# Windowed attention and a gelu MLP on one core: the order of work from the first down product on as one list of single-engine steps, with named PSUM banks

## The chip, the core and the metric

One core of a Trainium2 chip. The metric is device time in microseconds (us) of one launch, as the median of the runs. The engines are TensorE (PE, matmuls), VectorE (DVE), ScalarE (ACT), GpSimd (POOL) and SyncE (SP, which here only issues transfers). Each engine runs its own instructions in the order in which the kernel emits them and waits where it needs another engine's result.

## The reference

```
# q, k, v: 8 batches x 8 heads x 576 positions x 64
scores = q @ k^T / 8, kept where 0 <= i - j < 64, else -1e9
a      = softmax(scores) @ v
x      = a, as 4608 tokens x 512        # heads side by side
h      = x @ w_in                       # 512 -> 2048
g      = h * sigmoid(1.702 h)
out    = g @ w_out                      # 2048 -> 512, float32
```

## The kernel before

Matmuls are in bf16 with float32 sums in PSUM. The 4608 tokens are 36 tiles m of 128 and nine chunks of 512. A tile is two blocks of 64 queries, and each block sees 128 keys.

**Attention of a tile.** `scores` (L302, tag c in the list) takes 16 small matmuls with 64 rows of contraction into the two banks of pool psS, or "apart" into two single banks. `exp` (L327, x) makes the exponentials on ACT, `mask` (L337, m) multiplies by the band on DVE, `pv` or `pv_two` (L355 and L373, v) multiplies by values for one or two tiles into psT, and `norm` or `norm_two` (L360 and L384, n) divides on DVE. The rows are then turned to columns: for tiles below 16 by PE and copies (`x_mm` L411, `x_out` L434), above it by a transposing DMA on SP's queue (`x_dma` L436, xd).

**Loads for attention.** Batches 0 to 2 are loaded as float32 and cast. From tile (2, 3) on `load_bf16` (L226, l) loads q, k and v with casting DMAs on POOL's queue. `turn_dma` (L237, y) turns q and k by DMA on SP's queue, and `shift_v` (L231, h) makes the copy of v that is offset by half a block, on POOL. `v_nat` and `v_off` have two buffers each, by the parity of the batch, so a load of v for batch b writes over that of b - 2.

**MLP.** `up_mm` (L444, u) multiplies x by a part of w_in into one bank. g comes out of it in one of two ways: `up_gelu` (L483) on ACT alone, or `up_th` (L462) on ACT and then `up_g` (L478) on DVE. An exp after a gelu needs another table on ACT (`soften`, L1086). Chunk 0 goes down by plain products (`down` L486). The later half-chunks q (2 to 17) go down by a scheme of seven block products in place of eight: `add_g` (L534, a) and `add_w` form sums, `product` (L552, p) does n = 1, 6, 7, 4 into one bank (the chain) and 2, 5, 3 into another (the part), `keep_chain` (L588, k) copies a state of the chain away, `add_out` (L591, o) and `last_of_chain` (L597, z) put together the output, and `store` (L581, s) sends it. The last chunk's up products use the same scheme: `up_product` (L655, F), `up_keep` (K), `up_add` (O), `up_last` (G).

**Order.** The scheduler is off: each engine's order is the order of the calls. Up to a point in chunk 1 and 2 it is a list of calls written by hand; after it comes a text, `plan` (L1024), with 727 tokens such as `p2.1` or `u34.t`, which a loop (`steps`, L1121) turns into calls. Most tokens stand for steps on several engines: `l` for three loads, `y` for two turns, `t` for turns on PE and their copies on ACT, `u…g` for an up product and its gelu.

**Banks.** PSUM has eight banks: psS and psT have two each as one buffer, psH and psO two buffers of one bank each. A new tile takes the next buffer of its pool in turn and waits until that buffer's last readers are done. Outputs take one of five buffers of `ob_pool` in the same way.

Of the kernel before, what the change touches and what calls it, by code (L numbers as in the profile page):

```python
# [29 lines left out]
def kernel(  # L30
# [20 lines left out]
    ob_pool = ctx.enter_context(tc.tile_pool(name="ob", bufs=5))  # L51
    psS = ctx.enter_context(tc.tile_pool(name="psS", bufs=1, space=bass.MemoryType.PSUM))
    psT = ctx.enter_context(tc.tile_pool(name="psT", bufs=1, space=bass.MemoryType.PSUM))
    psH = ctx.enter_context(tc.tile_pool(name="psH", bufs=2, space=bass.MemoryType.PSUM))
    psO = ctx.enter_context(tc.tile_pool(name="psO", bufs=2, space=bass.MemoryType.PSUM))
# [30 lines left out]
    def load_v(b, i, queue=None):  # L86
        (queue or nc.sync).dma_start(
            out=heads(stage_of_v(b, i)[0 : size(i), :]), in_=rows_of(v, b, i)
        )

    def cast_v(b, i, engine=None, parts=(0, 1, 2)):
        n, vn, vo = size(i), v_nat[b % 2], v_off[b % 2]
        src = heads(stage_of_v(b, i)[:])
        pieces = [
            (vo[64:128, i, :, 0:D], src[0:64]),
            (vn[0:n, i, :, 0:D], src[0:n]),
            (vo[0:64, i + 1, :, 0:D], src[64:128]) if i < 4 else None,
        ]
        for p in parts:
            if pieces[p]:  # L100
                (engine or nc.gpsimd).tensor_copy(out=pieces[p][0], in_=pieces[p][1])
# [4 lines left out]
    def load_qk(b, i):  # L106
        for w, src in enumerate((q, k)):
            nc.sync.dma_start(
                out=heads(stage_of_qk(b, i)[0 : size(i), w, 0:DM]), in_=rows_of(src, b, i)
            )  # L110
# [4 lines left out]
    def cast_qk(b, i):  # L115
        n = size(i)
        for w in range(2):
            nc.gpsimd.tensor_copy(
                out=rows[b % 2][w][0:n, i, :], in_=stage_of_qk(b, i)[0:n, w, 0:DM]
            )  # L120

    def load_quads(half):
        hs = slice(4 * half, 4 * half + 4)
        for w, src in enumerate((q, k)):
            nc.sync.dma_start(
                out=stage_qk[half][:, w, :].rearrange("p (h e) -> p h e", h=4),
                in_=src[0, hs, 0:512, :].rearrange("h (p r) d -> p h (r d)", r=4),
            )
# [37 lines left out]
    def load_pairs(b, i):  # L166
        n = pairs(i)
        for w, src in enumerate((q, k)):
            nc.sync.dma_start(
                out=stage_qk[(3 * b + i) % 2][0:n, w, :].rearrange("p (h e) -> p h e", h=H),  # L170
                in_=src[b, :, 256 * i : 256 * i + 2 * n, :].rearrange(
                    "h (p r) d -> p h (r d)", r=2
                ),
            )
# [17 lines left out]
    def turn_mm(b, i, w, tiles):  # L192
        n = pairs(i)
        for hp in range(4):
            for r in range(2):
                nc.tensor.transpose(  # L196
                    out=tiles[hp // 2][:, w, hp % 2, r, 0:n],
                    in_=pair_rows(b, i, w)[0:n, hp // 2, r, P * (hp % 2) : P * (hp % 2) + P],
                    identity=ident[0:n, 0:n],
                )  # L200

    def turn_out(b, i, w, tiles, half, engine):
# [6 lines left out]
            in_=tiles[half][:, w, :, :, 0:n].rearrange("p g r n -> p g n r"),  # L209
        )  # L210

    def turn_tiles():

        return [
            pool.tile([P, 2, 2, 2, P], bf16, name="turn", tag=tag)
            for pool, tag in ((psS, "S"), (psT, "T"))
        ]

# [7 lines left out]
    def load_bf16(b, i):  # L226
        for w, src in enumerate((q, k)):
            nc.gpsimd.dma_start(out=heads(row_block(b, i, w)), in_=rows_of(src, b, i))  # L228
        nc.gpsimd.dma_start(out=v_nat[b % 2][0 : size(i), i, :, 0:D], in_=rows_of(v, b, i))  # L229

    def shift_v(b, i):  # L231
        vn, vo = v_nat[b % 2], v_off[b % 2]
        nc.gpsimd.tensor_copy(out=vo[64:128, i, :, :], in_=vn[0:64, i, :, :])  # L233
        if i < 4:
            nc.gpsimd.tensor_copy(out=vo[0:64, i + 1, :, :], in_=vn[64:128, i, :, :])  # L235

    def turn_dma(b, i):  # L237
        n = size(i)
        for w in range(2):
            nc.sync.dma_start_transpose(  # L240
                out=qkt[b % 2][w][:, :, PAD + P * i : PAD + P * i + n],
                in_=row_block(b, i, w),
            )
# [15 lines left out]
    for half in range(2):  # L259
        load_quads(half)  # L260
    for i in (0, 2):
        load_v(0, i)
    ident = keep.tile([P, P], bf16, name="ident")
    nc.gpsimd.memset(ident[:], 0.0)
    nc.gpsimd.affine_select(
        out=ident[:], in_=ident[:], compare_op=ALU.not_equal, fill=1.0,
        base=0, pattern=[[-1, P]], channel_multiplier=1,
    )
    band = keep.tile([P, 64], bf16, name="band")
    nc.gpsimd.memset(band[:], 1.0)  # L270
    nc.gpsimd.affine_select(
        out=band[:], in_=band[:], compare_op=ALU.is_ge, fill=0.0,
        base=64, pattern=[[1, 64]], channel_multiplier=-1,
    )
    nc.gpsimd.affine_select(
        out=band[:], in_=band[:], compare_op=ALU.is_ge, fill=0.0,
        base=-1, pattern=[[-1, 64]], channel_multiplier=1,
    )
    for i in range(2):
        nc.vector.memset(qkt[i][1][:, :, 0:PAD], 0.0)  # L280
        nc.vector.memset(v_off[i][0:64, 0, :, :], 0.0)
        nc.vector.memset(v_nat[i][:, :, :, D : D + 2], 2.0)
        nc.vector.memset(v_off[i][:, 1:5, :, D : D + 2], 2.0)
        nc.vector.memset(v_off[i][64:128, 0, :, D : D + 2], 2.0)

    band_all = keep.tile([P, 1024], bf16, name="band_all")
    nc.vector.tensor_copy(
        out=band_all[:].rearrange("p (n c) -> p n c", c=64),
        in_=band[:].unsqueeze(1).to_broadcast([P, 16, 64]),
    )  # L290
    far = keep.tile([P, 512], bf16, name="far")
    nc.vector.tensor_scalar(
        out=far[:], in0=band_all[:, 0:512],
        scalar1=-1.0, scalar2=30000.0, op0=ALU.add, op1=ALU.mult,
    )
# [6 lines left out]
    def scores(m, masked=False, apart=False):  # L302

        if apart:
            st = [psH.tile([P, 512], fp32, name="S", tag="H")[:] for _ in range(2)]
# [67 lines left out]
    def pv_two(m):  # L373

        acc = psT.tile([P, 2, 512], fp32, name="Tacc", tag="T")
        rest = psH.tile([P, 2, 66], fp32, name="Tacc", tag="H")
# [27 lines left out]
    def x_dst(m):  # L404
        ch = m // 4
        if m % 4 == 0:
# [21 lines left out]
    def x_out_two(m):  # L428
        ps = X_of.pop(m)
        for i in range(2):  # L430
            nc.scalar.copy(out=x_dst(m + i), in_=ps[:, i])

    def x_out(m):
        nc.scalar.copy(out=x_dst(m), in_=X_of.pop(m)[:])  # L434
# [7 lines left out]
    turns = itertools.count()  # L442

    def up_mm(ch, f, nf, t0, nt, wide=False):  # L444

        pool, tag = (psO, "O") if wide and next(turns) % 2 else (psH, "H")
        ps = pool.tile([P, nf, nt], fp32, name="hps", tag=tag)

# [37 lines left out]
    def down(ch, tsub, j, pool=None, tag="O"):  # L486

        if j == 0:
            O_of[ch, tsub] = (pool or psO).tile([P, DM], fp32, name="ops", tag=tag)
# [9 lines left out]
    def down_out(ch, tsub, on_dve=False):  # L499
        o_sb = ob_pool.tile([P, DM], fp32, name="o_sb", tag="o_sb")  # L500
        ps = O_of.pop((ch, tsub))
        if on_dve:
            nc.vector.tensor_copy(out=o_sb[:], in_=ps[:])
        else:
            nc.scalar.copy(out=o_sb[:], in_=ps[:])
        eng = nc.sync if ch < 6 else nc.scalar
        eng.dma_start(out=out_tiled[:, ch * 4 + tsub, :], in_=o_sb[:])
# [40 lines left out]
    def bank(c, pr, at, name):  # L548
        pool, tag = (psO, "O") if (c, pr) != (NCH - 1, 1) else ((psS, "S"), (psT, "T"))[at]
        return pool.tile([P, 256], fp32, name=name, tag=tag)  # L550

    def product(c, pr, n):  # L552
# [8 lines left out]
        if n == 1:  # L561
            A_of[c, pr] = bank(c, pr, 0, "chain")
        if n == 2:
            C_of[c, pr] = bank(c, pr, 1, "part")
# [11 lines left out]
    def out_half(c, pr, t, n):  # L576
        if (c, pr, t) not in o_of:
            o_of[c, pr, t] = ob_pool.tile([P, DM], fp32, name="o_sb", tag="o_sb")
        return o_of[c, pr, t][:, 256 * n : 256 * n + 256]

    def store(c, pr, t, half=None):  # L581
        eng = nc.sync if c < 6 or half == 1 else nc.scalar
        cols = slice(0, DM) if half is None else slice(256 * half, 256 * half + 256)
        eng.dma_start(
# [6 lines left out]
    def add_out(c, pr, n):  # L591
        at, t, half = {2: (0, 0, 0), 5: (2, 1, 1), 3: (1, 0, 1)}[n]
        nc.vector.tensor_tensor(  # L593
            out=out_half(c, pr, t, half), in0=C_of[c, pr][:], in1=kept(c, pr, at), op=ALU.add
        )

    def last_of_chain(c, pr, engine):  # L597
        copy_on(engine, out=out_half(c, pr, 1, 0), in_=A_of.pop((c, pr))[:])
# [49 lines left out]
    rings = itertools.count()  # L648
    homes = {32: "ST", 33: "H", 34: "ST", 35: "H"}

    def up_bank(g, at):
        pool, tag = (psH, "H") if homes[g] == "H" else ((psS, "S"), (psT, "T"))[at]
        return pool.tile([P, 2, 256], fp32, name="up", tag=tag)[:]

    def up_product(g, n):  # L655
# [523 lines left out]
```

The softmax here doesn't subtract the row's maximum and nothing guards it: scores larger than these inputs give would overflow.

## Time and profile before

| | |
|---|---|
| median of 3 runs | 295.6 us (294.55 to 295.86) |
| span of the profiled execution | 293.0 us |
| around the span (295.6 less 293.0) | 2.6 us |
| PE / DVE / ACT / POOL busy | 283.5 / 195.5 / 181.1 / 141.3 us |
| granted PE clock | 0.998 |
| last matmul ends | 289.7 us |

The span is from the first to the last instruction of one execution; the median is of executions without the profiler. Busy time of PE includes matmuls whose ends are modelled, so the starts are read where tenths of a microsecond matter. The mean DMA busy share is 90% or more in nearly every fortieth of the span until about 220 us; after that it falls.

### The profile page before, as it was taken

The page shows a single profiled execution, that of the slowest core. Times are in us where ns is not written, and L with a number is a line of the kernel's source. Part 1 is how long each engine was busy: PE and PEld are TensorE (multiplying, and loading weights), DVE is VectorE, ACT ScalarE, POOL GpSimd, SP SyncE. Part 2 cuts the span into 40 slices and gives each one's busy share as a digit, 9 for nine tenths or more (in the row PEclk, how much of TensorE's full clock was granted, in tenths as well). Part 3 has the DMA queues.
Part 4 walks back from the last instruction along what each step waited for, and adds up shares of the span by engine and source line. Part 5 has one row for each costly group of instructions (what it writes and reads, how often), then busy time and mean ns, then how long its engine had stood idle before and what let it go on. Part 6 is the DMA issues. An engine that isn't in the chain of part 4 may idle for free.

```text
span 293.0 us, 8976 instructions
## 1 busy us (share of the span) xinstructions
PE 283.5 (97%) x3783; PEld 249.6 (85%) x3783; DVE 195.5 (67%) x377; ACT 181.1 (62%) x289; POOL 141.3 (48%) x191
## 2 busy tenths in 40 slices
PE   7899999999999999999999999999999999999995
PEld 6578555999898898889898999998899899989984
DVE  5667715898898685375636573756787864768771
ACT  3676534877775389776758746776657653556411
POOL 1570446744999999709569985078510000000000
PEclk9999999999999999999999999999999999999999
DMA  7999999996999999999999999999955171001233
GB/s 237 236 206 219 240 243 225 239 159 128 84 142 119 166 130 134 185 164 146 140 186 154 139 151 198 183 160 143 142 70 117 36 182 39 0 2 72 74 125 126
DMA packets 149768, 42.79 MB, mean 146 GB/s; under 512 B 135136, under 2 KB 144864, under 8 KB 149728
## 3 DMA queue, kind: packets, MB, share of 16 engines
q0 software_dynamic: 77712, 13.64, 70.7%
q1 hardware_dynamic: 68208, 25.18, 49.4%
q10 hardware_dynamic: 3808, 3.41, 3.7%
q8 instruction: 29, 0.48, 0.7%
q14 instruction: 11, 0.09, 0.1%
HBM read 36.70 MB, written 9.44 MB: 157 GB/s over the span
## 4 chain that ended last, share of the span: by engine, by line
PE 78%; DMA 10%; DVE 4%; ACT 2%; SPq 2%; issue 2%; POOL 1%; ACTq 0%; DVEq 0%; POOLq 0%
PE hps L453 32%; PE chain L568 17%; PE part L568 13%; PE ops L491 5%; PE up L668 4%; DMA out_dram<-o_sb 3%; PE Tacc L347 3%; PE S L319 3%; DMA kt<-rows_k 3%; DMA stage_v<-in_v_dram 2%; DMA stage_qk<-in_k_dram 2%; SPq L240 1%; DVE stage_qk L528 1%; ACT PT L335 1%; PE turn L196 1%
## 5 line engine op out<-in xcount | busy, mean ns | idle before, releaser
L453 PEld LDWEIGHTS <-w_in_sb 128*128 128x128 bf16 x1312 | 109.6, 113 | 4.9 <-issue 0.7
L484 ACT ACTIVATE gT<-hps 128x512 bf16<-128x512 f32 x82 | 48.6, 597 | 34.5 <-PE hps L453 34.2
L453 PE MATMUL hps<-xT_pe,w_in_sb 128*128 128x128 bf16 (+2 forms) x800 | 61.0, 234 | 0.1
L453 PE MATMUL hps<-xT_dma,w_in_sb 128*128 128x256 bf16 x512 | 60.6, 273 | 0.3 <-ACT gT L694 0.3
L568 PEld LDWEIGHTS <-gT 128*128 128x128 bf16 x512 | 49.0, 98 | 5.9
L479 DVE SCALAR_TENSOR_TENSOR gT<-th,hps 128x512 bf16<-128x512 bf16 x46 | 30.8, 684 | 11.2 <-ACT th L464 11.0
L233 POOL COPY v_off<-v_nat 64x528 bf16<-64x528 bf16 x27 | 20.2, 752 | 33.9 <-DMA v_nat<-in_v_dram 33.1
L464 ACT ACTIVATE th<-hps 128x512 bf16<-128x512 f32 x46 | 27.0, 600 | 13.0 <-PE hps L453 12.6
L593 DVE TENSOR_TENSOR o_sb<-part,stage_v 128x256 f32<-128x256 f32 x48 | 20.2, 421 | 21.9 <-PE part L568 13.3
L335 ACT ACTIVATE PT<-S 128x1024 bf16<-128x1024 f32 x28 | 28.5, 1017 | 8.0 <-PE S L319 7.6
L339 DVE TENSOR_TENSOR PT<-PT,band_all 128x1024 bf16<-128x1024 bf16 x32 | 23.6, 748 | 5.6 <-ACT PT L335 5.4
L229 POOL DMA_DIRECT2D v_nat<-in_v_dram x27 | 23.5, 871 | 0.8 <-DMA rows_q<-in_q_dram 0.5
L228 POOL DMA_DIRECT2D rows_k<-in_k_dram x27 | 23.3, 865 | 0.3 <-DMA v_nat<-in_v_dram 0.3
L228 POOL DMA_DIRECT2D rows_q<-in_q_dram x27 | 23.1, 856 | 0.0
L568 PEld LDWEIGHTS <-sums 128*128 128x128 bf16 x192 | 18.6, 98 | 3.2 <-issue 1.1
L568 PEld LDWEIGHTS <-stage_v 128*128 128x128 bf16 x192 | 18.5, 98 | 2.2
L113 ACT COPY stage_v<-chain 128x256 f32<-128x256 f32 x22 | 8.2, 372 | 18.3 <-PE chain L568 18.3
L392 DVE TENSOR_TENSOR xs<-Tacc,rc 128x128 bf16<-128x128 f32 (+1 forms) x26 | 18.0, 692 | 0.9
L113 DVE COPY stage_v<-chain 128x256 f32<-128x256 f32 x26 | 10.9, 420 | 11.1 <-PE chain L568 10.9
L235 POOL COPY v_off<-v_nat 64x528 bf16<-64x528 bf16 x21 | 17.2, 820 | 1.2
L568 PE MATMUL chain<-stage_qk,sums 128*128 128x256 bf16 x128 | 16.6, 273 | 0.3 <-DVE stage_v L113 0.3
L568 PE MATMUL chain<-stage_qk,gT 128*128 128x256 bf16 x128 | 16.6, 273 | 0.0
(127 smaller groups left out, 450.6 us busy)
## 6 DMA issues: line engine op xcount, KB each, us to landing
out_dram<-o_sb SPq DMA_DIRECT2D x24, 256.0 KB, 4.7
rows_q<-in_q_dram POOLq DMA_DIRECT2D x21, 128.0 KB, 6.3
rows_k<-in_k_dram POOLq DMA_DIRECT2D x21, 128.0 KB, 6.7
v_nat<-in_v_dram POOLq DMA_DIRECT2D x21, 128.0 KB, 7.4
out_dram<-o_sb ACTq DMA_DIRECT2D x10, 256.0 KB, 2.1
stage_v<-in_v_dram SPq DMA_DIRECT2D x9, 256.0 KB, 6.7
stage_qk<-in_q_dram SPq DMA_DIRECT2D x4, 512.0 KB, 6.9
stage_qk<-in_k_dram SPq DMA_DIRECT2D x4, 512.0 KB, 8.0
```

The lines of the kernel that those rows point to most:

```text
L113: (nc.scalar.copy if engine is nc.scalar else engine.tensor_copy)(**kw)
L228: nc.gpsimd.dma_start(out=heads(row_block(b, i, w)), in_=rows_of(src, b, i))
L229: nc.gpsimd.dma_start(out=v_nat[b % 2][0 : size(i), i, :, 0:D], in_=rows_of(v, b, i))
L233: nc.gpsimd.tensor_copy(out=vo[64:128, i, :, :], in_=vn[0:64, i, :, :])
L335: nc.scalar.activation(out=e[:], in_=st[:], func=AF.Exp, scale=scale)
L339: nc.vector.tensor_tensor(out=pt, in0=pt, in1=band_all[:], op=ALU.mult)
L453: nc.tensor.matmul(ps[:, g, :], lhsT=w_in[:, c, (f + g) % 4 : 512 : 4], rhs=xT[ch][:, m0 : m0 + nt // P, c, :], start=(c == 0), stop=(c == 3),
L464: nc.scalar.activation(out=th[:], in_=ps[:], func=AF.Tanh, scale=1.702)
L479: nc.vector.scalar_tensor_tensor(out=g_of(*unit), in0=th[:], scalar=1.0, in1=ps[:], op0=ALU.add, op1=ALU.mult,)
L484: nc.scalar.activation(out=g_of(*unit), in_=ps[:], func=AF.Gelu_apprx_sigmoid, scale=2.0)
L568: nc.tensor.matmul(out[:, :], lhsT=left[:, j], rhs=right[:, j], start=new and j == 0, stop=j == 7, skip_group_check=True,)
L593: nc.vector.tensor_tensor(out=out_half(c, pr, t, half), in0=C_of[c, pr][:], in1=kept(c, pr, at), op=ALU.add)
```

## The change

The first part of the program keeps PE's order and its instructions. From the first `down` product on, the list written by hand and the plan are replaced by one flat list of 1286 tokens, in which every token is a step of one engine on one buffer.

- `psH` and `psO` (two buffers each) become four pools of one bank, a to d, and a step that starts a tile names its bank: `p.3.1.a`, `u.3.2.2.0.256.c`. `c.11.ab` are scores apart in banks a and b; S and T are as before.
- `ob_pool` with five buffers becomes five pools of one buffer, e to i, named by the first step that writes an output: `o.13.5.g`.
- Helpers are split: loads are `lb.b.i.q`, `.k` and `.v`, turns `y.b.i.0` and `.1`, shifts `h.b.i.0` and `.1`; the product, the tanh (`t`), the product with h (`g`) and the gelu (`e`) of an up unit are steps of their own; `X`, `Y`, `XX`, `YY` are a turn on PE and its copies.
- The order of the steps is new. Groups of scores often stand next to each other (`c.10 c.11.ab`, `c.17.ad x.17 c.16`), and value products next to turns.
- Nine up units that were tanh and product (46 before, 37 after) use gelu alone (82 and 91).
- Six copies of turned rows (`Y.5` to `Y.8`, `YY.14.0` and `.1`) go from ACT to DVE.
- Gelu and exp alternate more often: 27 loads of a table in place of 21.
- The first load of `load_bf16` stands right behind the first `down` products. Six shifts (`h.3.2.0`, `h.4.4.0`, `h.5.4.0`, `h.6.1.0`, `h.7.0.1`, `h.7.4.0`) come close behind the load of v that they read.
- The last steps (`p.17.4`, `z.17.A`, `s.17.1.0.A`) are as before.

```
-    ob_pool = ctx.enter_context(tc.tile_pool(name="ob", bufs=5))
+    ob0 = ctx.enter_context(tc.tile_pool(name="ob0", bufs=1))
...
+    obs = {"e": ob0, "f": ob1, "g": ob2, "h": ob3, "i": ob4}
...
-    psH = ctx.enter_context(tc.tile_pool(name="psH", bufs=2, space=bass.MemoryType.PSUM))
-    psO = ctx.enter_context(tc.tile_pool(name="psO", bufs=2, space=bass.MemoryType.PSUM))
+    psA = ctx.enter_context(tc.tile_pool(name="psA", bufs=1, space=bass.MemoryType.PSUM))
...
+    pools = {"S": psS, "T": psT, "a": psA, "b": psB, "c": psC, "d": psD}
...
-    def load_bf16(b, i):
-        for w, src in enumerate((q, k)):
-            nc.gpsimd.dma_start(out=heads(row_block(b, i, w)), in_=rows_of(src, b, i))
-        nc.gpsimd.dma_start(out=v_nat[b % 2][0 : size(i), i, :, 0:D], in_=rows_of(v, b, i))
...
+    def load_bf16(b, i, which):
+        if which == "v":
+            nc.gpsimd.dma_start(out=v_nat[b % 2][0 : size(i), i, :, 0:D], in_=rows_of(v, b, i))
+        else:
+            w = "qk".index(which)
+            nc.gpsimd.dma_start(out=heads(row_block(b, i, w)), in_=rows_of((q, k)[w], b, i))
...
-    def product(c, pr, n):
+    def product(c, pr, n, tag=None):
...
         if n == 1:
-            A_of[c, pr] = bank(c, pr, 0, "chain")
+            A_of[c, pr] = pools[tag].tile([P, 256], fp32, name="chain", tag=tag)
...
-        a4.3 a4.1 a4.2 o3.3 a4.4 u48.t u49.g p4.2 u50.g g48 l4.1 y4.1 u51.g u52.g u53.g k4.1.V o4.2
-        m15 s2.0 s3.0 m14 c16 x16 v14 n14 m16 c17.h x17 l4.2 p4.5 p4.6 k4.6.V t14 m17 u54.g p4.7 v16
...
-        G35.5 O34.5 p15.2 o15.2 k15.6.A p15.7 F35.3 a17.3.0 O35.3 F34.4 G34.5 F35.4 F34.3 s14.0
-        k15.7.V G35.3 G34.4 O34.3 G35.4 G34.3 p15.5 o15.5 s14.1 p15.4 z15.V a17.3.1 p15.3 o15.3
-        a16.3.1 a16.1.1 p17.1 k17.1.A a17.1.1 a17.2.1 a17.1.0 a16.2.1 a17.2.0 a17.4.0 p17.2 p16.1
...
+        lv.2.0.S lv.1.4.S cp.1.0.1.1.A cp.1.1.0.N.P cp.1.1.1.1.P cv.1.1.0.P d.0.1.0.d d.0.3.0.a
+        d.0.2.0.c tp.0.2.0.0 tp.0.2.1.0 op.0.2.0.0.V lp.1.2.0 tp.0.2.0.1 lb.2.4.q cv.1.2.1.P
...
+        lb.3.4.v o.2.2.i ds.0.2.S n.9.1 X.9.T p.2.5 y.3.1.0 y.3.3.1 k.2.7.V p.2.4 e.1.4.384 x.10
+        m.10 x.11 m.11 v.10.2.a o.2.5.g Y.9.A u.2.4.4.128.128.b t.2.4.128 y.3.0.0 h.2.4.0
...
+        p.4.5 e.3.12.0 a.6.3 y.4.1.0 a.6.1 e.3.8.256 z.4.V.f h.3.3.1 v.16.2.b y.4.0.1 c.19 c.18.ad
+        u.3.14.2.256.256.b a.5.2 e.3.6.256 u.3.10.2.256.256.a p.5.1.d o.4.5 n.16.2 xd.16 xd.17
...
+        e.4.8.256 m.20 v.20.2.c c.23.da y.4.4.0 lb.6.2.v y.4.4.1 c.22 k.7.7.V p.7.4 s.6.0.N.S a.8.3
+        a.8.1 a.8.2 u.4.2.2.256.256.d x.23 m.23 lb.4.4.v h.4.4.0 s.5.0.N.S p.8.1.a n.20.2 p.7.2.c
+        k.8.1.A p.8.6 s.6.1.N.S h.5.1.0 o.7.2.i lb.5.3.v z.7.V.f p.7.5 y.5.2.1 k.8.6.V p.8.7 o.7.5
+        p.7.3 x.22 m.22 v.22.2.b lb.6.1.q e.4.2.256 y.5.2.0 c.24 y.5.3.1 y.5.3.0 c.25.dc x.24
...
+        u.5.0.2.256.256.c e.5.8.0 a.10.3 a.10.1 xd.24 p.9.7 c.28 k.9.7.V y.6.0.0 c.27.ac p.8.5
+        s.7.0.N.S p.9.4 e.5.2.256 e.5.12.256 xd.25 u.6.2.2.0.256.a a.8.4 e.5.0.256 a.11.3 o.8.5
...
+        o.14.3 s.14.0.N.A p.15.2.d o.15.2.e G.35.5 F.35.3 p.16.2.b F.34.3 O.34.3 G.34.3 O.35.3
+        G.35.3 p.15.5 o.15.5.g a.16.3.1 a.16.1.1 s.11.1.N.S a.16.2.1 p.15.4 p.17.1.S k.17.1.V
...
     for step in plan.split():
-        name, *args = step[0], *step[1:].split(".")
-        steps[name](*(int(a) if a.isdigit() else a for a in args))
+        name, *args = step.split(".")
+        steps[name](*(int(a) if a.isdigit() else None if a == "N" else a for a in args))
```

## The prediction

> **What bounds the kernel now.** I read the page's busy shares first, then the chain that ended last, then TensorE's (PE's) timeline and its waits, and the transfers last.
>
> ```profile
> PE 283.5 (97%) x3783; PEld 249.6 (85%) x3783; DVE 195.5 (67%) x377; ACT 181.1 (62%) x289; POOL 141.3 (48%) x191
> PE 78%; DMA 10%; DVE 4%; ACT 2%; SPq 2%; issue 2%; POOL 1%; ACTq 0%; DVEq 0%; POOLq 0%
> ```
>
> PE is busy 97% of the span, and the chain runs 78% through it. VectorE (DVE) and ScalarE (ACT) have about 100 us of slack each, so work on them counts only where PE waits for a result. The last matmul ends at 289.7 of 293.0; the 3.3 us after it are an ACT copy and a store, which the change leaves as they are. What the change can do is alter the time between PE's first `down` product and its last matmul. There PE does the same multiplications in both versions; the order decides how often PE changes its array shape and how often it waits.
>
> PE's timeline prices a change of shape (start, duration, engine, line):
>
> ```profile
> 126.84 1.04 PE L568 MATMUL part<-w_out_sb,gT 128*128 128x256 bf16 x8
> 127.81 0.41 PE L319 MATMUL S<-qt,kt 64*128 64x64 bf16 x16
> 128.15 1.05 PE L568 MATMUL chain<-stage_qk,stage_v 128*128 128x256 bf16 x8
> ...
> 138.62 0.64 PE L319 MATMUL S<-qt,kt 64*128 64x64 bf16 x32
> 139.19 1.05 PE L568 MATMUL chain<-stage_qk,gT 128*128 128x256 bf16 x8
> ```
>
> Read the starts; the durations overlap. Between equal shapes a product of eight matmuls of 256 columns takes 0.873 us from start to start. The one at 126.84 gives way to scores (64*128) only after 0.97, 0.10 more. The single group of scores lasts 0.34. Two groups in one visit last 0.57, so the second adds 0.23, and 0.34 - 0.23 = 0.11 is what leaving the shape costs. A change of shape is about **0.105 us**.
>
> PE's waits, the four that lie after the first `down` (us in total, times, longest):
>
> ```profile
> PE S L319 <- DMA kt<-rows_k: 0.5, 1, 0.5
> PE part L568 <- DVE o_sb L593: 0.5, 1, 0.5
> PE hps L453 <- ACT gT L694: 0.3, 1, 0.3
> PE chain L568 <- DVE stage_v L113: 0.3, 1, 0.3
> ```
>
> That is 1.6 us by this view. From start to start, which includes the refill of the pipeline, the four are 0.65 (at 122.6), 0.49 (256.2), 0.46 (90.5) and 0.50 (204.4), so 2.1; shorter holes at 79.1, 81.4, 102.5 and 107.9 add 0.5. PE waits for others for **2.6 us** in all.
>
> **What the skill says.** The Trainium skill, "TensorE: Matmul & The Clock Gate", section "Back-to-back issue gap", gives N/2.4 + 2.5 ns between matmuls of N columns: 109.2 for 256. The trace agrees (0.873/8 = 109 ns), so there is nothing inside a product to win. "TensorEngine Tiling (Array Packing)", section "Key Properties", says that a switch of tiling mode drains the array; the 0.105 us agree. "Trainium Kernel Development and Optimization", section "Key Constraints", says that the transfers of all queues interleave on the same 16 DMA engines; the trace agrees, since turned blocks (`xd`), median 5.9 us from issue to landing, take 7.7 between 110 and 120, while POOL's loads come in a burst. "ScalarE: Activation LUTs", section "What ACT_TABLE_LOAD costs", prices a table switch at 1.28 us and a drain of about 1.38; the trace shows 1.28, and no drain:
>
> ```profile
> 76.82 0.61 ACT L434 COPY xT_pe<-pxt 128x512 bf16<-128x512 bf16 x1
> 77.44 1.28 ACT L484 ACT_TABLE_LOAD   x1
> 79.31 0.60 ACT L484 ACTIVATE gT<-hps 128x512 bf16<-128x512 f32 x1 [0.59 <-PE hps L453]
> ```
>
> The load starts as the copy ends, and the gelu behind it still waits 0.59 for PE: the switch was hidden.
>
> **The change part by part.**
>
> *Named banks and buffers, single-engine steps.* The counts of banks (eight) and output buffers (five) stay, and no instruction is added for a name. Names only decide which earlier reader a tile waits for, so their cost is in the waits below. By themselves: 0.
>
> *Work moved between engines.* Nine pairs of tanh (ACT 0.60) and product with h (DVE 0.68) become one gelu (ACT 0.60): DVE -6.2. Six copies of turned rows go from ACT (0.59) to DVE (0.69): ACT -3.5, DVE +4.1. Table loads go from 21 to 27: six times 1.28, plus the small activation before an exp, ACT +8.3. ACT becomes about 186 and DVE 193 of 293: neither bounds. Hidden behind PE, hence 0; without cover a table load costs up to 1.3 each, 7.7 for six.
>
> *PE's order.* I wrote both lists out as PE's instructions and counted changes of shape after the first `down`: 84 before, 68 after, because scores are put beside scores (`c.10 c.11`) and value products beside turns; visits away from the full array go from 36 to 27. 16 x 0.105 = **-1.7**. Bounds: 0 if grouped work shares no drain, -1.8 at 0.11 each.
>
> *PE's present waits.* The places are taken apart by the new order: **-2.6** if each is covered. Bounds -2.6 and 0.
>
> *New waits on DVE and ACT.* I looked at every product of the new list for what it needs and how much PE work lies between. Latencies from the trace: PE's end to an ACT or DVE start 0.20, ACT to DVE 0.03, DVE or ACT to PE 0.05. Worst is `p.17.1`, which takes bank S after `G.35.3`. From the end of `F.34.3`: 0.20 + O.34.3 0.69 + O.35.3 0.69 + 0.03 + G.35.3 0.63 + 0.05 = 2.29, against two products (1.75) on PE: 0.54. Before, three products (2.6) covered it. Three more in the last stage (`F.33.7` after `K.33.6.A`, `p.13.3` after `o.13.5.g`, `F.35.3` after `O.35.5`) come to about 0.2 each. **+1.2**, bounds 0.3 and 2.
>
> *New waits for transfers.* This is where the trace of before can't show the answer, since the queues are filled differently. POOL's single loads (`lb`) are spread from about 45 us on, by their place in the list, where `load_bf16` began at 73; both end near 210. For each reader on PE I took the PE work since its transfer could start, and took off the latencies, issue (about 1.2 us on SP, 0.87 on POOL) and shifts that lie between. The rest is the landing time that it tolerates:
>
> - `c.26` after `y.5.4.1`: 5.0 us; `c.27` after `y.6.0.0`: 4.8
> - `u.4.8.0` after `xd.17`: 5.2
> - `v.22` after `lb.4.4.v` and its shift, then `h.5.1.0`: 5.4; that load itself waits until `v.20` has freed the buffer that `lb.6.2.v`, ahead of it, fills.
>
> The rows of the transfers (the last number is the median from issue to landing):
>
> ```profile
> qt<-rows_q SPq DMA_TRANSPOSE x30, 5.7
> kt<-rows_k SPq DMA_TRANSPOSE x30, 5.7
> v_nat<-in_v_dram POOLq DMA_DIRECT2D x6, 64.0 KB, 6.1
> xT_dma<-xs SPq DMA_TRANSPOSE x20, 5.9
> ```
>
> At the medians the four are late by 0.7, 0.9, 0.7 and 0.7: 3.0 us. At the faster quarter (4.1 to 5.1) next to nothing is. With loads thinner I take **+1.0**, bounds 0 and 3 (the burst is a rival).
>
> *Sum.* -1.7 - 2.6 + 1.2 + 1.0 = **-2.1**. The profiled execution has a span of 293.0 and about 2.6 us around it, which is the median of the runs, 295.6. So 295.6 - 2.1 = **293.5 us**, by a span of 290.9.
>
> **Rivals.**
>
> *The landings eat the gain.* If transfers take their medians, +3.0 stands for +1.0: -1.7 - 2.6 + 1.2 + 3.0 = -0.1, **295.5** (296.3 with engine waits at their bound of 2). For it: the DMA engines are at 90% or more in most slices to 220 us. Against it: moved bytes are the same and start earlier.
>
> *Slower: POOL waits for its own load.* This queue runs in order, and in the trace it is already held:
>
> ```profile
> POOL v_off L233 <- DMA v_nat<-in_v_dram: 33.1, 7, 11.5
> ```
>
> Seven waits, the longest 11.5 us, each with later loads behind it. In the new list six shifts (`h.3.2.0`, `h.4.4.0`, `h.5.4.0`, `h.6.1.0`, `h.7.0.1`, `h.7.4.0`) stand close behind the load that they need, so a late landing holds the following loads, which then go out in a burst. With landings as in the burst of before (7.5 for `y`, 7.7 for `xd`, 9 to 10 for v) `c.26` is late by 2.6, `c.27` by 2.9, `u.4.8.0` by 2.5, `v.22` by some 4, `u.5.4.256` after `xd.23` (tolerates 6.3) by 1.4: 13 us, of which one delay lets the next transfer land and about half remains. -4.3 + 1.2 + 6.5 = +3.4, **299.0**. It decides once new waits exceed 4.3 us (no gain) by 1.5. Uncovered table loads would do the same with 7.7 - 2.1: 301; against it stand 100 us of slack on ACT and 46.8 us that ACT waited for PE ahead of gelu and tanh (34.2 + 12.6).
>
> *It doesn't do what it says.* If the order gained nothing because PE's time is all multiplication (holes merely move): **295.6**, in the "same" case.
>
> *Better.* If all waits vanish: -4.3 + 0.3, **291.6**.
>
> **How the numbers follow.** A difference of 0.5%, 1.5 us, is about what a measurement of this kernel can tell from no change; faster begins below 294.1. My forecast with the better case has 0.50, the eaten gain and the empty order together 0.27, POOL's mechanism with the table loads 0.23. The range runs from 290.8 (the best case, less 0.7 for the scatter of the three runs, 294.55 to 295.86) to 298.0, half of the slower case left out. The likeliest case's own range is 291.5 to 294.5.
>
> **What would show it.** PE's last matmul near 287.6 instead of 289.7. Two groups of scores in one visit at some 0.57 us, fewer changes of shape. In PE's waits the old `S <- DMA kt` at 122.6 gone, and a new one at `p.17.1` of about 0.5 on ACT's gT. POOL's wait for v_nat below 33 us and transfers landing at 5.7 or sooner. The forecast is wrong if PE's waits for `kt`, `xT_dma` or `v_off` sum to over 3 us, if ACT_TABLE_LOAD stands ahead of a matmul in the chain, or if the granted clock differs from before's 0.998.

## The result and the profile after

The changed kernel takes 302.9 us (median of 4 runs, 300.8 to 304.5) where the kernel before takes 295.1 (4 runs). The ratio is **1.027**, 95% interval 1.021 to 1.032: slower by some 8 us, where 293.5 was forecast. A ratio leaves out the runs that took over 1.5% longer than the fastest of the same kernel, while medians are of all runs. The profiled execution took 304.5, with a span of 302.8 and a mean TensorE clock of 0.988.

First the busy shares and the head of the chain, from the page of the changed kernel:

```profile
PE 284.9 (94%) x3783; PEld 251.0 (83%) x3783; DVE 191.0 (63%) x372; ACT 183.4 (61%) x299; POOL 138.1 (46%) x191
PE 58%; DMA 10%; SPq 3%; DVE 2%; issue 0%; ACT 0%; ACTq 0%
```

The second line has to be read with care: its shares sum to some 73%, since this chain was followed back only to 76 us. What counts is the first: PE does the same work in a longer span, 94% busy in place of 97%. DVE and ACT are below two thirds and PE's new waits for them come to 1.2 us (in the ledger below), so the work moved between them isn't the reason. PE's waits in the changed kernel (us in total, times, longest) name it:

```profile
PE hps L447 <- DMA xT_dma<-xs: 5.6, 3, 2.5
PE S L318 <- DMA qt<-rows_q: 3.9, 1, 3.9
PE idle L692 <- POOL ident L268: 1.4, 1, 1.4
```

The `kt`, `o_sb` and `gT` waits of before are gone. Four waits for turned rows have come: one before a group of scores, three before up products. The third line is the start of the program and was there before. The chain of waits, in order of time, shows the first and the last of the four:

```profile
88.64 0.39 SPq L242
...
89.12 1.22 SPq L242
...
90.47 1.21 SPq L242
...
91.71 2.32 SPq L242
...
94.14 5.57 DMA qt<-rows_q
99.71 0.14 issue
99.85 0.64 PE S L318 x32
100.49 1.39 PE chain L559 x8
101.88 1.71 PE hps L447 x16
103.59 1.30 PE part L559 x8
```

```profile
215.17 7.38 DMA xT_dma<-xs
222.55 0.14 issue
222.68 4.25 PE hps L447 x24
226.94 1.07 PE chain L559 x8
```

SP issues one turn after another, 1.2 us or more each. The last of them is `y.2.3.0`, at 94.1; it lands at 99.7, and the scores `c.12` start at 99.85. PE had nothing to do for 4.04 us from start to start, 3.9 by the view of its waits. The other three are `u.5.4.256` behind `xd.23` (2.41 us, landing 8.7 us after issue), `u.6.2.0` behind `xd.25` (1.07; 6.6) and `u.6.2.256` behind `xd.26` (2.66; 7.4). Together **10.2 us**, from start to start.

Then look at the lines *after* the waits. Twenty-four matmuls of 256 columns take 4.25 us by this chain, 4.05 from start to start, where they take 2.62 elsewhere; a product takes 1.39 and 1.30 where it takes 0.87. From 100.87 to 104.28 and from 223.8 to 227.2 matmuls start at twice their distance: PE runs at **half speed** for 3.4 us, twice. That adds 3.3 us. The trace also records the clock that PE was granted. In these two windows of time the first numbers are the length and PE's busy time in us, and the third from the right is the clock:

```profile
97.50:100.91 3.41, 1.06 (x37) 1.00 (x38) 0.00 (x0) 0.64 (x2) 1.92 (x3) 1.00 2.30 185
100.91:104.32 3.41, 3.41 (x27) 2.88 (x25) 1.45 (x3) 2.06 (x4) 0.91 (x2) 0.50 2.06 150
```

The record has a clock of 0.5 from 100.91 to 104.32 and again from 223.79 to 227.20, and 1.0 elsewhere up to the last matmul.

The ledger of PE's last matmul, from starts in the two traces: it ends at 299.3 in place of 289.7, +9.6. Waits for turned rows +10.2, half speed +3.3, old waits -2.6, new waits on DVE +1.2 (0.65 at `p.2.6`, 0.39 at a score at 57.9, two of 0.1), changes of shape -2.1: +10.0, which closes to 0.4.

### The profile page after: what moved, and what is told of

Its sections match the earlier page's. It is cut to its first block, busy times and chain, and to the rows that moved or that the text cites. A ratio compares the mean times of both kernels' runs of the same rounds, so it can differ in the third digit from the quotient of the medians.

```text
span 302.8 us, 8961 instructions
## 1 busy us (share of the span) xinstructions
PE 284.9 (94%) x3783; PEld 251.0 (83%) x3783; DVE 191.0 (63%) x372; ACT 183.4 (61%) x299; POOL 138.1 (46%) x191
## 3 DMA queue, kind: packets, MB, share of 16 engines
q10 hardware_dynamic: 3808, 3.41, 3.7%
## 4 chain that ended last, share of the span: by engine, by line
PE 58%; DMA 10%; SPq 3%; DVE 2%; issue 0%; ACT 0%; ACTq 0%
PE hps L447 22%; PE chain L559 15%; PE part L559 12%; DMA xT_dma<-xs 7%; PE up L658 4%; PE Tacc L346 2%; SPq L242 2%; PE S L318 2%; DMA qt<-rows_q 2%; DVE xs L391 1%; DMA out_dram<-o_sb 1%; SPq L434 1%; PE pxt L423 0%; ACT o_sb L117 0%; DVE o_sb L583 0%
## 5 line engine op out<-in xcount | busy, mean ns | idle before, releaser
L447 PEld LDWEIGHTS <-w_in_sb 128*128 128x128 bf16 x1312 | 110.8, 114 | 11.8 <-issue 5.4
L478 ACT ACTIVATE gT<-hps 128x512 bf16<-128x512 f32 x91 | 51.1, 597 | 40.3 <-PE hps L447 40.1
L447 PE MATMUL hps<-xT_dma,w_in_sb 128*128 128x256 bf16 x512 | 62.6, 277 | 5.6 <-DMA xT_dma<-xs 5.6
L447 PE MATMUL hps<-xT_pe,w_in_sb 128*128 128x128 bf16 (+2 forms) x800 | 62.0, 236 | 0.0
L559 PEld LDWEIGHTS <-gT 128*128 128x128 bf16 x512 | 49.7, 99 | 6.1
L473 DVE SCALAR_TENSOR_TENSOR gT<-th,hps 128x512 bf16<-128x512 bf16 x37 | 25.0, 683 | 16.3 <-ACT th L458 16.3
L458 ACT ACTIVATE th<-hps 128x512 bf16<-128x512 f32 x37 | 21.8, 594 | 13.8 <-PE hps L447 13.7
L237 POOL COPY v_off<-v_nat 64x528 bf16<-64x528 bf16 x27 | 17.4, 656 | 26.2 <-DMA v_nat<-in_v_dram 25.7
L334 ACT ACTIVATE PT<-S 128x1024 bf16<-128x1024 f32 x23 | 23.4, 1019 | 7.1 <-PE S L318 6.9
L239 POOL COPY v_off<-v_nat 64x528 bf16<-64x528 bf16 x21 | 15.9, 772 | 13.4 <-DMA v_nat<-in_v_dram 13.0
L318 PEld LDWEIGHTS <-kt 64*128 64x128 bf16 x576 | 9.8, 95 | 8.9 <-issue 7.9
```

What stands on the lines that cost most here:

```text
L334: nc.scalar.activation(out=e[:], in_=st[:], func=AF.Exp, scale=scale)
L447: nc.tensor.matmul(ps[:, g, :], lhsT=w_in[:, c, (f + g) % 4 : 512 : 4], rhs=xT[ch][:, m0 : m0 + nt // P, c, :], start=(c == 0), stop=(c == 3),
L458: nc.scalar.activation(out=th[:], in_=ps[:], func=AF.Tanh, scale=1.702)
L473: nc.vector.scalar_tensor_tensor(out=g_of(*unit), in0=th[:], scalar=1.0, in1=ps[:], op0=ALU.add, op1=ALU.mult,)
L478: nc.scalar.activation(out=g_of(*unit), in_=ps[:], func=AF.Gelu_apprx_sigmoid, scale=2.0)
L559: nc.tensor.matmul(out[:, :], lhsT=left[:, j], rhs=right[:, j], start=new and j == 0, stop=j == 7, skip_group_check=True,)
```

## The experiments

**Theory** after this profile: the order itself gains what was forecast; its turned rows come late because of the place of single transfers in SP's and POOL's in-order queues, and half speed follows from the idle PE. **Rivals:** POOL waiting for its own loads, which then crowd the DMA engines; readers too close behind their turns whatever the traffic; an order that costs time by itself. All ratios are to the kernel before on the same chip, whose median was 295.1 to 296.0, so gains between experiments are safer by the ratios than by the microseconds. Intervals are 95%.

**1. Turns of batch 2 first.**

```
-  y.2.4.1 y.3.0.1 ... y.3.1.0 y.3.3.1 ... y.3.0.0 ... y.2.3.1 ... y.2.4.0 ... y.2.3.0
+  y.2.4.1 y.2.3.1 y.2.3.0 y.2.4.0 y.3.0.1 ... y.3.1.0 y.3.3.1 ... y.3.0.0
```

> Edit: y.2.3.1, y.2.3.0 and y.2.4.0 (turns of batch 2, needed by c.12) move on SP's queue from behind five turns of batch 3 to right behind y.2.4.1; nothing else changes. Theory (SP's order): c.12 waited 4.04 us at 95.7 because its last turn was issued only at 94.1, behind y.3.0.1, which itself waited for its load; moved ahead, the wait at c.12 goes (-4.0) and so does the half-speed stretch of TensorE at 100.9 to 104.3 that follows it (-1.7): about 297.2 where the change measured 302.9. Rival (landings are slow because POOL's loads crowd the DMA engines): the turn lands just as late or the stall moves to the next reader, and the time stays within 1.5 us of 302.9. Rival (the stall is real, the half-speed stretch has another cause): 298.9, with the stretch still there.

Measured: 299.1, ratio 1.010 (1.007 to 1.013). The wait at `c.12` is gone, and no half-speed stretch follows there. A score pair at 103.7 now waits 1.3 us for a turn further back, and the three waits for `xT_dma` stay (5.2 us). The place in SP's queue was the cause at `c.12`; of the forecast 5.7 us, 3.8 came (5.0 by the ratios, 1.027 to 1.010).

**2. POOL not held by `lb.6.2.v`.**

```
-  v.20.2.c c.23.da y.4.4.0 lb.6.2.v y.4.4.1 ... lb.6.2.q
+  v.20.2.c c.23.da y.4.4.0 y.4.4.1 ... lb.6.2.q lb.6.2.v
```

> Edit: the load lb.6.2.v, which holds POOL from 144.6 to 161.4 until v.20 frees its buffer, moves behind eight later steps of POOL (to behind lb.6.2.q); nothing else changes. Theory (blocked queue, then a burst): the nine loads that POOL sent off at 168 to 176 in one burst go out earlier, xd.22 and xd.23 land in about 5 us where they took 7.2 and 8.7, and the wait of 2.41 us at 178.5 goes: 302.9 - 2.4 = 300.5. Rival (the reader u.5.4.256 stands too close behind xd.23 whatever the traffic): landing stays above 7.5 us and the time at 302.9. Rival (POOL's wait carries further turns too): more than 4 us go.

Measured: one of four runs at 296.1, three at 302.5 to 303.8, so no ratio is given. PE's waits in its profiled execution, which took 303.8:

```profile
PE S L318 <- DMA qt<-rows_q: 5.5, 2, 4.2
PE S L318 <- DMA kt<-rows_k: 1.9, 1, 1.9
```

None of the three waits for `xT_dma` that the theory spoke of is left, but besides `c.12` two score groups now wait for turns, at 171.7 and 217.7, and a new 1.57 us lies at `u.4.8.0`. By these waits the crowd moved to other transfers, and the edit fits neither theory's number.

**3. Idle matmuls in the stall.**

```
-  c.12.bc
+  warm.60.b c.12.bc
```

> Edit: 60 matmuls of the identity (3.3 us of TensorE work whose result is not used) are put in front of c.12, inside the stall of 4.04 us at 95.7. Theory (the half-speed stretch at 100.9 to 104.3 comes from the idle TensorE before it): c.12 starts when it did, the stretch goes, -1.7: 301.2, granted clock about 0.993. Rival (the stretch is drawn by something else, the load of the DMA engines or chance): stretch and time stay, 302.9. If the stall is shorter in a run than 3.3 us, the added work costs the difference.

Measured: 300.7 (4 runs), ratio 1.018 (1.009 to 1.026). PE's timeline at the place (start, duration):

```profile
95.69 1.04 PE L559 MATMUL part<-w_out_sb,gT 128*128 128x256 bf16 x8
96.56 3.51 PE L692 MATMUL idle<-ident 128*128 128x128 bf16 x60
100.13 0.64 PE L318 MATMUL S<-qt,kt 64*128 64x64 bf16 x32
100.70 1.05 PE L559 MATMUL chain<-stage_qk,stage_v 128*128 128x256 bf16 x8
101.59 1.06 PE L447 MATMUL hps<-xT_pe,w_in_sb 128*128 128x128 bf16 x16
```

The scores start no later than they did against the product before them, and the sixteen matmuls after them take 0.89 from start to start where they took 1.71. All four runs have a mean clock of 0.998 or more; of eight runs of the changed kernel (four more are below) six lie at 0.986 to 0.994. Half speed comes from the idle PE: the clocks and the trace show it, while the ratio alone, with an interval that ends at 1.026 against 1.027, would not.

The clock records of all eighteen kernels of this study say how. They have ten stretches at half speed before the last matmul, nine of 3.41 us and one of twice that (experiment 13). In each trace the edges of these records lie on one grid of 3.41 us: in the changed kernel the second stretch starts 122.88 us after the first, 36 times 3.413. Cut each trace into windows on its grid and add up PE's idle time in each. All six windows with 2.0 us or more are followed by a window at half speed, of the seven with 1.65 to 1.95 five are, and none with less. So it is not the length of a wait alone that counts, but how much of it falls into one window. At `u.6.2.256` PE waited 2.6 us in experiment 1 and 2.5 in the changed kernel. In experiment 1 the wait fell into two windows as 1.4 and 1.2, and the clock stayed; in the changed kernel 2.3 fell into one, and the clock was halved.

The Trainium skill, "TensorE: Matmul & The Clock Gate", section "Part 1: The HAM clock gate (the "warmup" mystery)", gives a free-running window of 3.41 us and a half-rate clock after an idle window. The length agrees (100.91 to 104.32), and so does the grid. That a whole window must be idle does not: PE was busy for 1.06 of the 3.41 us ahead of the first stretch, and the measurement decides. In the kernel before, whose runs show a lower clock less often, 11 of 39 runs beside experiments 1 to 4 had a clock of 0.994 or less, with a median of 297.2 against 295.6 for the others.

**4. Shifts behind the next loads.**

```
-  lb.3.2.v h.3.2.0 ... lb.3.2.q p.3.6 lb.3.4.q
+  lb.3.2.v lb.3.2.q lb.3.4.q h.3.2.0 ... p.3.6
...
-  lb.5.4.v ... h.5.4.0 ... lb.6.3.k lb.6.3.q
+  lb.5.4.v ... lb.6.3.k lb.6.3.q h.5.4.0
```

The edit shows two of the places. At the first of them the two loads go ahead of three further shifts too. `h.4.4.0` and four shifts of batches 6 and 7 move in the same way.

> Edit: the shifts h that stand right behind the load of v that they read go behind the next loads (h.3.2.0 behind lb.3.2.q and lb.3.4.q, h.4.4.0 behind lb.5.3.v, h.5.4.0 behind lb.6.3.q, h.6.1.0, h.7.0.1, h.7.0.0 and h.6.1.1 behind lb.6.4.v). Slower rival of the prediction (POOL waiting for its own load makes the bursts that delay TensorE): POOL's waits for v_nat fall from 38.7 us to below 20 and 3 us or more go: below 300. Theory now (the stalls come from SP's order and from the one load lb.6.2.v): TensorE's four stalls stay, 301.5 to 303.

Measured: 298.1 (20 runs), ratio 1.006 (1.003 to 1.009): 4.8 us went (6.2 by the ratios), and the theory of that moment was wrong. POOL's waits for v, and two more:

```profile
POOL v_nat L229 <- issue: 22.1, 2, 14.3
POOL v_off L237 <- DMA v_nat<-in_v_dram: 11.1, 6, 3.2
POOL v_off L239 <- DMA v_nat<-in_v_dram: 10.7, 4, 4.4
```

In the changed kernel the last two were 25.7 and 13.0, so 38.7 became 21.8, where below 20 was expected. `c.12` still waits (3.3), the three waits for `xT_dma` fall from 6.1 in all (start to start) to 1.7, though one of 1.0 appears at `u.4.8.0`. The prediction's slower rival, POOL held by its own load, was at work.

**5 and 6. Both orders without turned rows.** Both kernels have the same edit:

```
-  lhsT=src[1][part, hp, 64 * j : 64 * j + 128], ...
+  lhsT=(src[1][part, hp, 64 * j : 64 * j + 128] if b < 3 else w_in_sb[0][part, hp, 0:128]), ...
-  rhs=xT[ch][:, m0 : m0 + nt // P, c, :],
+  rhs=(xT[ch][:, m0 : m0 + nt // P, c, :] if not 4 <= ch < 8 else w_out_sb[:, c, 0:nt]),
```

> Edit to the changed kernel: scores of batches 3 to 7 and up products of chunks 4 to 7 read weights (w_in_sb, w_out_sb) in place of the turned rows; all transfers and all instructions stay, in the same order, but no matmul of these waits for a turn (the output is another one). Theory (the order itself gains what was forecast, and the turned rows take it back): the waits of 10.2 us but for c.12 (batch 2, 4.0, stays unless the turns go faster) and one half-speed stretch of 1.7 go: 302.9 - 6.2 - 1.7 = 295.0, and 289.5 if c.12 is in time as well. Rival (the order costs time by itself, by engine waits or shapes): 299 or more.

> The same edit to the kernel before: its scores and up products read weights in place of turned rows. It waited 0.5 us for a turn: theory, 295.1 - 0.5 = 294.5, so that the two orders, both without turns, stand as forecast (the new one 4 to 5 us faster once c.12 is left out). Rival (turns cost the kernel before as well, by its order around them): below 293.

Measured: the changed order 298.0 (4 runs), ratio 1.013 (1.006 to 1.020); the order before 294.6, ratio 0.998 (0.995 to 1.000). The second is as forecast. The first is 3 us above it: its profiled execution took 296.1, with `c.12` at 2.5 and one stretch of half speed, and the other runs lie higher. The two longest, 298.5 and 299.4, have a clock of 0.988 against its 0.994, which is one more window at half speed, 1.7 us; the rest this trace can't show. These two did not settle what the order is worth.

**7 and 8. Edits 1 and 4 together, and every other stall besides.** In 7, `y.3.0.0` also goes right behind `y.3.0.1` and `y.3.3.1` behind `y.3.2.0`. In 8, further:

```
-  xd.24 p.9.7 c.28 k.9.7.V y.6.0.0 ... s.7.0.N.S ... xd.25
+  xd.24 xd.25 p.9.7 c.28 k.9.7.V y.6.0.0 ... s.7.0.N.S
-  y.7.1.1 ... n.26.2 ... y.6.4.0 ... xd.27 ... xd.26
+  n.26.2 xd.27 xd.26 y.7.1.1 ... y.6.4.0
```

> Both single edits that helped, together: the turns of batch 2 ahead of those of batch 3 (here also y.3.0.0 right behind y.3.0.1 and y.3.3.1 behind y.3.2.0, by first reader), and the shifts behind the next loads. Theory (two separate places, c.12 and POOL's bursts): the gains add, -3.8 and -4.8 from 302.9: 294.3. Rival (both shorten the same queue, so the second gives little): 297 to 298.

> As the one before, and besides: xd.25 right behind xd.24, xd.27 and xd.26 right behind n.26.2 (ahead of y.7.1.1 and y.6.4.0), and on DVE w.3.0 and w.4.0 behind k.2.1.V and k.2.6.V. Theory: the waits at u.6.2.0 (1.07), u.6.2.256 (2.66, with a half-speed stretch of 1.7) and p.2.6 (0.65 to 1.67) go as well: 294.3 - 4 to 5 = 290, faster than the kernel before. Rival (a turn moved ahead makes the one behind it late by the same): no better than the one before.

Measured: 7 at 294.4, ratio **0.998** (0.996 to 1.001); 8 at 296.5, ratio 1.007 (1.003 to 1.011). In microseconds the two gains add up as forecast (8.5 of 3.8 and 4.8). By the ratios, which compare on one chip, they come to 8.4 where the two alone make 11.2, about three quarters. In the profiled execution of 7 the last wait for a turn is

```profile
PE hps L447 <- DMA xT_dma<-xs: 1.5, 1, 1.5
```

at `u.6.2.0`. In 8 this one is gone, but scores behind the turns that were passed over wait 1.7 us at 185.8 and 0.6 twice at 214: a turn moved ahead on SP makes the one behind it late.

**9 and 10. The changed kernel again, and one place of edit 4 alone.** In 10 only `h.6.1.0`, `h.7.0.1`, `h.7.0.0` and `h.6.1.1` go behind `lb.6.4.v`.

> The changed kernel once more, as the reference for the others on this chip: 302.9 as before (ratio 1.027), with the waits at c.12, u.5.4.256 and u.6.2.256 and one to three half-speed stretches.

> Edit to the changed kernel: only h.6.1.0, h.7.0.1, h.7.0.0 and h.6.1.1 go behind lb.6.4.v; the other moves of the run with later shifts are left out. Theory (a shift that waits for its own load holds the loads behind it, and these then land together with xd.27 and xd.26): the wait at u.6.2.256 (2.66 us at 219.9) goes, and the half-speed stretch of 223.8 to 227.2 with it (-1.7); c.12, u.5.4.256 and u.6.2.0 stay: 302.9 - 4.4 = 298.5. Rival (the gain of the later shifts came from the earlier places): 301.5 or more, and the wait at u.6.2.256 stays.

Measured: 9 at 302.4, ratio 1.025 (1.019 to 1.031); 10 at 301.1, ratio 1.024 (1.017 to 1.030). In 10 the wait at `u.6.2.256` is gone, as expected, but the total hardly moved: `c.12` (2.4), `u.5.4.256` (2.1), `u.6.2.0` (1.1) and three score groups of 0.5 to 0.8 wait, and a half-speed stretch has come at 179. So most of what experiment 4 gained came from its earlier places. In 9 all four named places wait, with other sizes than in the first trace (2.6, 1.8, 1.8, 1.6, and 0.9 at a score). The sizes vary with the transfers of each execution; the places stay.

**11. Scores apart.** Version 7 with eight scores moved back by one product:

```
-  c.24 y.5.3.1 y.5.3.0 c.25.dc ... u.4.14.2.256.256.b
+  c.24 y.5.3.1 y.5.3.0 ... u.4.14.2.256.256.b c.25.dc
```

> Edit to the version with turns and shifts moved (ratio 0.998): eight scores that stand next to other scores (c.11, c.13, c.16, c.18, c.22, c.25, c.27, c.31) move one product back, so that TensorE makes 16 more changes of array shape; nothing else changes. Theory (0.105 us for each): +1.7 us, ratio 1.004, and in the trace about 0.2 more for each pair. Rival (the price of a change of shape hides in other waits, and grouping gains nothing): ratio below 1.000. Rival (scores made later cost more through exp and mask behind them): +3 or more.

Measured: 297.0, ratio 1.007 (1.004 to 1.010), 2.6 us over version 7. In the trace, 16 more changes from and to scores cost 1.8 us, 0.11 each; the rest is in waits behind the later exps, 0.7 of it at one up product (`PE hps` for ACT's `PT` at 124).

**12. Version 7 mended.** `y.6.0.0` behind `y.6.1.1`, where SP was idle, `xd.25` behind `xd.24`, `w.4.0` behind `k.2.1.V`.

> Edit to the version with turns and shifts moved: y.6.0.0 goes to behind y.6.1.1, where SP's queue was idle, xd.25 right behind xd.24, and w.4.0 behind k.2.1.V on DVE. Theory: the waits at u.6.2.0 (1.7) and p.2.6 (0.6) that were left go: 294.4 - 2.0 = 292.4, ratio 0.991, faster than the kernel before. Rival (the waits move to the next turn): ratio 0.998 or more.

Measured: 293.8 (22 runs), ratio **0.995** (0.993 to 0.998), faster than both kernels. The two waits are gone; a score pair at 109.7 waits 1.6.

**13 and 14. Thin loads.** The same edit in both kernels:

```
+  def share(b, i):
+      return slice(0, 1 if b >= 4 and i > 0 else H)
-  nc.gpsimd.dma_start(out=heads(row_block(b, i, w)), in_=...)
+  nc.gpsimd.dma_start(out=heads(row_block(b, i, w))[:, share(b, i)], in_=...[:, share(b, i)])
```

> Edit to the changed kernel: POOL's loads of q, k and v of batches 4 to 7 (all but the first block of each batch) bring one head of eight; the rest of each buffer keeps older values, so the output is another one. Instructions, order and waits stay. Theory (transfers crowd one another): xd.23, xd.25 and xd.26 land in 2.4 to 4 us, and their three waits (2.4, 1.1, 2.7 us) with one half-speed stretch (1.7) go; c.12, which lies before these loads, stays with 4.0 + 1.7: 302.9 - 7.9 = 295.0. Rival (place in SP's queue and too near a reader, whatever the traffic): at least two of the three waits stay, 299 or more.

> The same edit to the kernel before. Theory: it waits only 0.5 us for a turn, so at most 1 us goes, 294 to 295; c.12's stall left out, the changed order with thin loads then stands about 4 to 5 us below it in TensorE time. Rival (the kernel before also loses to the crowd, in ways its waits don't show): below 293.

Measured: the changed kernel 294.5 (20 runs), as forecast to 0.6 us, and 293.1 for the eleven runs over which its ratio of 0.994 (0.991 to 0.996) is taken; the kernel before 294.4, ratio 0.998 (0.995 to 1.000). PE's longest wait of the changed one, and its turns (the last number is the median us to landing):

```profile
PE S L321 <- DMA qt<-rows_q: 4.4, 1, 4.4
```

```profile
qt<-rows_q SPq DMA_TRANSPOSE x30, 3.1
kt<-rows_k SPq DMA_TRANSPOSE x30, 2.7
xT_dma<-xs SPq DMA_TRANSPOSE x20, 2.8
```

`c.12`, ahead of the thin loads, waits as ever. All three waits for `xT_dma` are gone, with no instruction moved: the turns issued between 160 and 215 land in 2.3 to 4.4 us where they took up to 8.7. **They were late because POOL's loads crowded them.** With thin loads the two kernels are level by their medians although one still pays for `c.12`. In the two traces PE's last matmul ends at 292.8 and 289.3; without `c.12` (4.6 from start to start) and the half speed that starts with its scores (2.4 by the starts) the changed order would end at 285.8, 3.5 us ahead. The forecast for the order without transfers was -1.7 - 2.6 + 1.2 = -3.1. This agrees, but it is a subtraction in one execution, of 297.8 us, and not a time that was measured.

**15 and 16. One gating load ahead; POOL freed.** Version 12 with `lb.3.4.k` right behind `lb.3.4.q` and `y.3.4.0` behind `y.3.4.1`; 16 has edit 2 besides.

> Edit to the version of ratio 0.995: lb.3.4.k goes right behind lb.3.4.q and y.3.4.0 behind y.3.4.1, since y.3.4.1 held SP's queue until 102.6 for this load, and a score at 109.7 then waited 1.8 us. Theory (a load that gates the head of SP's queue): the wait goes, 293.8 - 1.5 = 292.3, ratio 0.990. Rival (the transfers of that stretch are crowded in any order): ratio 0.995 as before.

> As the one before, and lb.6.2.v goes behind lb.6.2.q, as in the second run. Theory (POOL no longer held from 142 to 160, so its loads no longer burst beside xd.22 and xd.23): the 1.0 us at u.5.4.256 goes, ratio 0.987. Rival (as in the second run, the loads that go out earlier make turns of batch 5 and 7 late): ratio above 0.992.

Measured: 15 at 292.7 (12 runs), ratio **0.991** (0.988 to 0.995); 16 at 293.2 (22 runs), ratio 0.992 (0.990 to 0.994). The wait at 109.7 is gone as forecast. In 16 `u.5.4.256` no longer waits, but it gains nothing that these intervals can show. Version 15 has the lowest median of the study, 2.5 us below the kernel before, and 16 lies within its interval.

## Why the prediction was wrong, by its own steps

*Changes of shape, -1.7.* Right in kind and nearly in size: -2.1 in the trace, a little beyond the bound of -1.8, and taking eight pairs apart cost 1.8 in the trace of experiment 11.

*Present waits, -2.6.* Right: the old places no longer wait. (The wait for `kt` that the prediction looks for at 122.6 stood at 204.4; the one at 122.6 was for `o_sb`. Both are gone.)

*New waits on DVE and ACT, +1.2.* The size was right by luck. `p.17.1` and the three other places of the last stage did not wait at all. The 1.2 that came are at 57.9, at `p.2.6`, whose copy `k.2.1.V` stands on DVE behind four sums of weights, and in two holes of 0.1.

*Work moved between engines and table loads, 0.* No PE wait on ACT showed up in the changed kernel's profile, so the cover held. This was read from the profile, not tried on its own.

*New waits for transfers, +1.0, bounds 0 and 3.* **This is the step that failed.** It measured +10.2, in three ways.

- The list of places was wrong. `c.26`, `c.27`, `u.4.8.0` and `v.22` did not wait in the profiled execution. `c.12`, `u.6.2.0` and `u.6.2.256` did and were not on the list: I had reckoned each transfer from when its data was ready. But SP's queue takes 1.2 us for a turn and stands still at one whose load hasn't landed, and `y.2.3.0` was behind five turns of batch 3 (experiment 1).
- The landing time was a median over the whole run. In the changed kernel the medians are even lower than before (`xT_dma` 5.0 against 5.9), and yet the landings ahead of close readers are 6.6 to 8.7. For `u.5.4.256` the tolerance of 6.3 us that the rival named was exact: 8.7 - 6.3 = 2.4, the wait measured. What was wrong was the landing put in.
- The bound of 3 took "thinner loads" for granted. POOL stood from 144.6 to 161.4 on `lb.6.2.v`, a hold that the prediction named but did not price, and then sent off nine loads from 167.5 to 177, beside `xd.22` and `xd.23`.

*Not in the sum at all:* half speed, +3.3. The prediction priced a wait at its length. Here the two long ones cost 1.6 to 1.7 us more each.

*The slower rival* had the right mechanism: POOL held behind its own loads, landings of 7 to 9 us, time lost at PE. Experiments 4 and 13 show it. But it put the losses at the wrong readers, all but `u.5.4.256`, and its 299 left out `c.12` and half speed. The rival of table loads without cover showed nowhere, nor did an order that gains nothing: with the crowded transfers out of the way the order is worth about what was forecast by the subtraction in experiments 13 and 14, and 2.5 us as a measured time in 15. The eaten gain with the empty order (0.27) and the slower rivals (0.23) were given half the chance between them; the range, which ended at 298, left out the half of the slower case in which the result lies.

*What stays open:* what besides the clock puts most runs of experiment 5 above the profiled one, why two of the seven windows with 1.65 to 1.95 us of idle PE were not followed by half speed, and how much of the 3.1 us a kernel with all its transfers can keep.

## What to carry to other kernels

When a list of steps is reordered, replay the in-order DMA queues too, with their issue times and the step at which each stands still, before asking how late a transfer may land. Take landing times from the crowd expected at that moment, not from a median, and keep a queue from standing still and then sending everything at once. A wait that leaves TensorE idle for 2 us or more of one 3.41 us window cost its length and up to 1.7 us of half-speed work besides, so two small waits are cheaper than one long one of the same sum.

## What the runs showed of the hardware

A turn of 128x512 lands 2.4 us after issue when little else is under way (the fastest of all 20 `xT_dma`), and took 7.2 and 8.7 us (`xd.22` and `xd.23` of the changed kernel) when 13 and 15 other transfers were under way for some part of that time. TensorE's clock was halved for 3.41 us, on a grid of this length, after each of the six windows of the grid in which it had been idle for 2.0 us or more and after none with less than 1.65; 60 useless matmuls in the wait at `c.12` prevented it there (experiment 3).
